# Three spectra exchanged by matmul instead of by DMA, in a gated sum of two spectral filters, under a new instruction list

## The chip, the cores and the metric

One core of a Trainium2 chip runs the whole program in one launch. The metric is the device time of that launch in microseconds. The core has five engines that each run their own instructions in order and wait for each other by semaphores: TensorE (PE, matmul; its weight loads are shown as PEld), VectorE (DVE), ScalarE (ACT), GpSimd (POOL) and SyncE (SP, which here only issues DMAs). Matmuls write to PSUM, an accumulation memory of eight banks that GpSimd cannot read; everything else lies in SBUF, the 128-partition working memory.

## The reference

```python
def reference(A_x, A_w_r, A_w_i, B_x, B_w_r, B_w_i, gate_w):
    x = A_x                                   # (1, 2048, 1024) bf16
    g = sigmoid((x * gate_w).sum(-1, keepdims=True))
    a = irfft2(rfft2(x) * (A_w_r + 1j*A_w_i)) # over both axes, W is (2048, 513)
    b = irfft2(rfft2(x) * (B_w_r + 1j*B_w_i))
    return g * a + (1 - g) * b                # bf16
```

Two filters act on the same two-dimensional spectrum of x, and a gate per row mixes the two results.

## The kernel before, in words

Both transforms are matrix products with constant cosines and sines. The 2048 rows are split as 32 x 64, so that the forward transform goes in steps; the work is cut into *jobs*, each a small function that adds one or a few instructions.

- **fold, egen, s1m, s1e**: stage 1. x arrives in eight groups (load.x.g.half), is folded or reversed (fold), and meets a constant E (two halves, load.E) of which egen makes signed copies. s1m.g.j are eight matmuls into one PSUM unit, s1e.g.j evicts that unit into F1 (line 458). There are 16 of these pairs.
- **s2m, s2e, s4m, s4e**: for each of 16 values t (in the order 1 to 12, 0, 13, 14, 15) eight matmuls transform along the columns (s2m), an eviction stores to one of three CS buffers (s2e), four matmuls with constants from CK finish the row transform (s4m, line 490), and an eviction gives the spectrum X(t) (s4e, line 498). Partition 2k holds the real, 2k+1 the imaginary part.
- **swap, xneg**: the complex product needs the spectrum with real and imaginary rows exchanged as well. swap(t) does it with two DMAs from SBUF to SBUF (line 502), into S(t). xneg(t) makes the copy with alternating signs (line 507), XN(t); the second half of XN(t) overwrites the first half of S of the spectrum four steps earlier, so it waits until that has been read by prod2.
- **prod1, prod2, pm**: the products with the weights W, read from memory in chunks (load.W), on VectorE. prod1 reads XN, prod2 reads S. Block 0 is the low 256 columns for one t (blocks 3 and 4 are its halves); pm does the high columns for several t at once.
- **gwm, gwe, gsm, gse, rowsum, zsm, zse, zst, zld**: the gate: a few matmuls beside stage 2, sums over t, a sigmoid, a round trip through memory into SI.
- **stm, ste, stp, stx, c0m, c0e**: the one column at the Nyquist frequency and column 0, put in order separately.
- **s5m.g, s5e.g** (g = 0 to 31): sixteen small matmuls and an eviction each turn the products round. s5m of g below 16 waits for the low products, of g from 16 for the first half, and of g from 24 for the second half of the pm products.
- **rb**: multiplies the inverse constants U5 by the gate SI. There are eight, for four groups of rows and two parts (cs) each; s6m.p needs both parts of its rows.
- **s6m, s6e, s7m, s7c, s7p, fin, store**: the inverse transform by blocks of rows i = 0 to 15. s7c copies half of a PSUM unit, s7p adds and subtracts on VectorE, fin combines the two halves, store writes out. The mode per i is `"QDQQDQQDQQDQQHHH"`; in mode D (i = 1, 4, 7, 10) s7p writes part of its result into PSUM. PQ, what fin reads, is a ring of four.

Two things set the order of the work. One is the written list ORDER (line 19): its jobs are emitted in that order, each engine runs its own in list order, and a suffix names the engine (a ScalarE, d VectorE, p GpSimd, s SyncE; the same letter on load, swap and store names the queue). The other is the helper that turns what each job reads and writes into semaphore waits; PSUM is four units that are handed out in the order in which the list gives them back (lines 333 to 342).

```python
def take(*key):
    unit_of[key] = free.pop(0)
    return unit_of[key]
```

All matmuls are recorded on line 330, ScalarE's copies on 316 and with signs on 325, VectorE's casts on 318, sign passes on 327, products and rb on 321, DMAs on 312, egen.1.2 on 425, folds on 436, s7p on 728, 729 and 737, fin on 747.

Of the kernel before, what the change touches and what calls it, by code (L numbers as in the profile page):

```python
# [18 lines left out]
ORDER = """
load.SM.a load.x.0.1.s load.x.1.1.s zero load.x.0.0.a load.E.0.a load.x.1.0.s load.x.2.0.a load.x.2.1.s wf.5 wf.1 wf.4 load.E.1.s fold.0.1.p  # L20
wf.2 tbl fold.0.0.d warm.10x512x1 load.x.4.0.s egen.0.1 fold.1.0.d load.x.4.1.a fold.1.1.d s1m.0.1 load.x.7.0.s s1m.0.0 fold.2.1.d
fold.2.0.d load.GR.p s1m.1.1 egen.1.3 egen.1.1 load.x.6.1.a load.x.7.1.a load.x.5.1.s load.x.6.0.a fold.4.0.d s1e.0.1.a s1m.1.0 wf.3
s1e.1.1.a s1m.2.1 wf.6 egen.1.2 rev s1e.2.1.a s1m.4.1 s1m.4.0 load.x.5.0.s s1e.1.0.d s1e.0.0.a load.VC.p fold.7.0.d load.x.3.0.s s1m.2.0
load.x.3.1.s s1m.7.0 fold.6.0.d load.F2.s s1e.4.0.a load.W.9.4.s fold.5.0.p s1m.6.0 load.CK.s s1e.2.0.d s1m.6.1 s1e.4.1.a fold.3.0.d
s1e.7.0.a s1e.6.0.a s1m.5.1 s1e.6.1.a fold.3.1.d s1m.5.0 s1e.5.1.a s1m.3.0 s1e.5.0.d s1m.7.1 s1m.3.1 gwm s1e.3.0.a s1e.7.1.d s1e.3.1.a s2m.1
s2e.1.a s2m.2 gwe.a load.W.24.4.s s2m.3 load.W.0.5.s s2e.3.a s2e.2.d s4m.1 s4e.1.a s2m.4 s4m.2 s2m.6 load.W.28.4.s s4m.3 s2e.4.a gsm.1.4
xneg.1.a s4e.2.d s4m.4 load.W.5.4.s gse.1.4.a swap.1.s s2e.6.d s4e.3.a swap.2.a s4e.4.d xneg.3.a s2m.5 swap.3.s s2m.7 s2e.7.a s2m.9 s4m.6
s2e.5.d gsm.5.4 swap.4.a load.W.20.4.s xneg.4.d s2e.9.a s4m.7 prod1.3.0.d gse.5.4.a prod1.4.0.d s4e.6.a s4m.5 prod2.1.0.d s2m.10 gsm.0.1
swap.6.s s4e.7.a prod2.3.0.d prod2.2.0.d s4e.5.a s4m.9 xneg.6.d prod1.1.0.d s2e.10.a s2m.8 xneg.2.p swap.7.a gse.0.1.a swap.5.s xneg.7.d
s2e.8.a load.W.16.4.s s4m.10 s4e.10.a s4e.9.a s2m.11 s4m.8 s4e.8.a gsm.9.4 gse.9.4.a s2e.11.a prod2.4.0.d xneg.5.d prod1.2.0.d swap.9.s  # L30
gsm.13.3 swap.8.a prod1.7.0.d s2m.12 prod1.5.0.d prod2.6.0.d prod1.6.0.d swap.10.s load.W.13.3.s prod2.5.0.d xneg.10.d xneg.9.d prod2.7.0.d
s2e.12.a xneg.8.d s2m.0 prod1.9.0.d s4m.11 gse.13.3.a s2e.0.a prod1.8.0.d s4m.12 rowsum.0.p s4e.12.a s4e.11.d s4m.0 s2m.13 swap.12.s stm
s2m.14 s4e.0.a swap.11.s xneg.11.d rowsum.1.d prod2.8.0.d rowsum.2.d s2e.13.a prod2.9.0.d xneg.12.d xneg.0.d prod1.12.0.d prod1.11.0.d
s2m.15 s2e.14.a prod2.10.0.d s4m.13 s2e.15.a prod2.12.0.d prod1.10.0.d prod1.0.3.d prod1.0.4.d s4m.15 ste.d s4e.13.a s4m.14 zsm swap.0.s
s4e.15.a stp.2 swap.13.s s4e.14.a xneg.15.a xneg.13.d prod2.11.0.d prod2.0.0.d stp.1 prod1.13.0.d swap.14.a prod2.13.3.d stx.p swap.15.s
prod1.15.4.d prod1.15.3.d zse xneg.14.a prod1.14.3.d prod2.15.3.d prod2.14.3.d prod1.14.4.d s5m.5 prod2.13.4.d s5e.5.a prod2.15.4.d
pm.1.0.0.13.3.d pm.1.1.0.9.7.d pm.1.1.1.9.7.d s5m.1 s5m.3 s5e.1.a s5m.7 s5e.3.a s5m.6 prod2.14.4.d zst.p s5e.7.a s5m.14 s5m.2 pm.1.0.0.5.8.d
s5e.6.a stp.0 s5e.14.a pm.1.1.1.1.8.d pm.1.0.1.1.4.d s5m.12 pm.1.0.1.13.3.d s5m.8 pm.1.0.1.5.8.d prod2.0.1.d c0m s5e.2.a c0e.d s5e.8.a
s5e.12.a s5m.9 pm.1.1.0.1.8.d s5m.0 pm.1.0.0.1.4.d s5m.4 s5e.9.a pm.2.1.1.9.7.d prod1.0.2.d s5m.13 s5m.15 s5e.0.a prod1.0.1.d pm.2.0.0.5.8.d
s5e.15.a pm.2.0.1.13.3.d s5m.10 s5e.10.a s5m.11 s5m.19 s5e.4.a s5e.11.a prod2.0.2.d pm.2.0.1.1.4.d s5e.13.a s5m.22 s5e.22.a s5m.17 zld.s  # L40
s5e.19.a s5m.23 s5e.23.a s5m.21 pm.2.1.0.1.8.d s5e.21.a pm.2.0.0.13.3.d pm.2.1.0.9.7.d pm.2.1.1.1.8.d pm.2.0.0.1.4.d pm.2.0.1.5.8.d s5m.20
load.U5.0.s s5m.16 s5e.20.a s5e.17.d s5m.18 s5m.27 load.U5.1.s s5e.18.a s5m.26 s5m.28 s5e.16.d rb.0.4.1.p s5e.27.a s5e.26.d s5e.28.a s5m.24
s5m.31 s5m.29 s5m.30 s5e.24.d s5m.25 s5e.31.a rb.0.4.0.p load.DI.s s5e.29.a s5e.30.d s5e.25.a s6m.0.0 rb.4.4.0.d s6m.1.0 s6m.0.1 rb.4.4.1.d
s6e.0.0.a s6e.1.0.a s6m.1.1 rb.8.4.0.d s6e.0.1.a s6m.2.0 s7m.0 rb.12.4.1.d rb.8.4.1.d s7c.0.a s6e.1.1.d s7m.1 rb.12.4.0.d s6e.2.0.a
s7p.0.0.d s7p.0.1.d fin.0.1.p fin.0.0.p s7c.1.a s7m.2 s7c.2.a s7p.1.1.d s6m.2.1 s6m.3.1 s7p.2.0.d s7p.2.1.d s7m.3 s6e.2.1.a s7p.1.0.d
s6m.3.0 s6e.3.1.a fin.1.0.d s7c.3.a fin.1.1.d fin.2.1.p s7m.4 store.0.0.a s6e.3.0.a s7c.4.a s7p.3.0.d s7p.3.1.d s7p.4.1.d s7m.5 s7c.5.a
s6m.4.0 fin.2.0.p s6m.4.1 s7p.5.0.d s7p.5.1.d s7m.6 s7p.4.0.d s6e.4.0.a s6e.4.1.a fin.3.0.p s7c.6.a fin.4.0.d s7m.7 s6m.5.0 store.0.1.a
fin.4.1.d fin.3.1.p fin.5.1.p store.1.1.s s6m.5.1 store.3.0.s store.2.0.s fin.5.0.p s7c.7.a store.1.0.a s7p.6.0.d s7p.6.1.d s6e.5.0.a
s7p.7.1.d s7p.7.0.d s7m.8 s6e.5.1.a fin.7.0.d s7m.9 s6m.6.0 s7c.8.a fin.7.1.d store.5.0.a s7c.9.a s7p.8.0.d s7p.8.1.d store.2.1.s
store.4.0.s s6m.6.1 s7m.10 s6e.6.0.a store.7.0.a s7p.9.0.d s6m.7.0 fin.6.1.p fin.6.0.p store.3.1.p s7p.9.1.d s7c.10.a store.6.0.a fin.8.1.p  # L50
s7m.11 s7p.10.1.d s6e.6.1.a s7m.12 s7p.10.0.d s6e.7.0.a store.5.1.s store.7.1.s fin.10.0.d fin.8.0.p s7c.11.a s6m.7.1 fin.9.0.p fin.10.1.d
fin.9.1.p s7p.11.0.d s7p.11.1.d s7c.12.a store.8.0.a s6e.7.1.a store.4.1.a store.6.1.s s7m.13 fin.11.0.d s7p.12.0.d fin.11.1.p s7c.13.a
s7p.12.1.d fin.12.0.p fin.12.1.p store.8.1.a store.10.0.a store.10.1.s s7m.14 store.9.1.s s7c.14.a store.9.0.s store.11.1.a store.12.1.p
s7m.15 store.11.0.a s7p.13.0.d s7p.13.1.d s7p.14.0.d s7c.15.a store.13.0.a s7p.14.1.d s7p.15.0.d s7p.15.1.d store.13.1.s store.14.1.s
store.12.0.p store.14.0.a store.15.0.s store.15.1.a
"""


# [202 lines left out]
def bass_gated_mix__spectral_gfnet__spectral_gfnet__prompt_kernel(nc, A_x, A_w_r, A_w_i, B_x, B_w_r, B_w_i, gate_w, out):  # L261
# [52 lines left out]
    def copy(eng, dst, src, **kw):  # L314
        if eng == "act":
            P.add("act", lambda e: e.activation(dst, src, ACT.Copy), **kw)  # L316
        else:
            P.add(eng, lambda e: e.tensor_copy(dst, src), **kw)  # L318
# [4 lines left out]
    def sign(eng, dst, src, col, **kw):  # L323
        if eng == "act":
            P.add("act", lambda e: e.activation(dst, src, ACT.Copy, scale=SM[:, col:col + 1]), **kw)  # L325
        else:
            P.add(eng, lambda e: e.tensor_scalar(out=dst, in0=src, scalar1=SM[:, col:col + 1], scalar2=None, op0=ALU.mult), **kw)  # L327

    def mm(o, lh, rh, first, last, **kw):
        P.add("pe", lambda e: e.matmul(o, lh, rh, start=first, stop=last), **kw)  # L330
# [500 lines left out]
```

## Time and profile before

| | us |
|---|---|
| runs shown | 123.19 (median), 127.07, 123.03 |
| profiled execution | 122.19 |
| its span, first to last instruction | 120.4 |
| busy: PE, DVE, ACT, POOL | 102.4, 101.5, 91.9, 42.6 |
| mean granted TensorE clock | 0.972 of full speed |

The page of the profile gives busy time by engine, the chain of work that ended last, and groups of instructions by line and shape: "x30" is a count, a bracket with an arrow names what ended the idle time ahead of an instruction. A merged row of the timeline gives the start of the first instruction, the time to the end of the last and their number. Consecutive instructions of one engine overlap a little, so that the spacing from start to start is shorter than the duration of one.

### The profile page before, as it was taken

How to read it: one execution, taken by the hardware profiler on the slowest of the kernel's cores; microseconds unless marked ns; L12 is line 12 of the kernel's file. 1: busy time of each engine (PE TensorE's matmuls, PEld its weight loads, DVE VectorE, ACT ScalarE, POOL GpSimd, SP SyncE). 2: the span in 40 equal slices, each digit the busy share in tenths (PEclk: the TensorE clock that was granted, in tenths of full speed). 3: DMA queues.
4: the chain of work that ended last, by engine and by line, in shares of the span. 5: the costliest groups of instructions: out<-in, count | busy, mean ns of one | idle time of the engine just before them, and what ended most of it. 6: DMA issues, size and time to landing. Idle time of an engine off the chain costs nothing.

```text
span 120.4 us, 3373 instructions
## 1 busy us (share of the span) xinstructions
PE 102.4 (85%) x1387; PEld 81.4 (68%) x1395; DVE 101.5 (84%) x165; ACT 91.9 (76%) x111; POOL 42.6 (35%) x40
## 2 busy tenths in 40 slices
...
GB/s 30 343 353 384 380 420 407 419 420 415 391 302 320 283 277 308 290 166 251 16 0 5 166 338 155 419 155 0 5 0 5 21 66 89 265 204 62 265 198 238
DMA packets 13535, 26.58 MB, mean 221 GB/s; under 512 B 2288, under 2 KB 6416, under 8 KB 13136
## 3 DMA queue, kind: packets, MB, share of 16 engines
...
q0 software_dynamic: 384, 0.55, 1.3%
...
## 4 chain that ended last, share of the span: by engine, by line
PE 55%; DVE 29%; DMA 5%; POOL 3%; ACT 2%; issue 2%; SPq 1%; POOLq 0%
PE PS L330 55%; DVE PF L321 23%; DMA PF<-in_A_x_dram 5%; POOL PF L747 2%; ACT PF L316 2%; DVE PF L318 1%; DVE PF L327 1%; SPq L312 1%; DVE PF L436 1%; DVE WA L318 1%; ACT PF L425 1%; DVE AT L595 0%; POOL out_dram L312 0%; POOLq L770 0%; DVE PST L321 0%
## 5 line engine op out<-in xcount | busy, mean ns | idle before, releaser
L316 ACT ACTIVATE PF<-PS 128x1024 bf16<-128x1024 f32 (+1 forms) x69 | 59.7, 929 | 15.0 <-PE PS L330 13.7
L330 PE MATMUL PS<-PF 128*128 128x256 bf16 (+2 forms) x404 | 51.2, 281 | 4.1 <-POOL PF L358 1.3
L330 PEld LDWEIGHTS PS<-PF 128*128 128x128 bf16 x406 | 36.5, 99 | 16.4 <-issue 2.4
L321 DVE TENSOR_TENSOR PF<-PF,WA 128x1024 bf16<-128x1024 bf16 (+4 forms) x62 | 39.8, 706 | 0.1
L330 PE MATMUL PS<-CK,PF 128*128 128x64 bf16 x512 | 21.4, 204 | 7.9 <-DVE PF L321 4.8
L316 ACT ACTIVATE WA<-PS 128x1024 bf16<-128x1024 f32 x27 | 25.3, 1062 | 3.5 <-PE PS L330 3.4
L330 PEld LDWEIGHTS PS<-CK,PF 128*128 128x128 bf16 x512 | 19.8, 120 | 9.4 <-DVE PF L321 5.3
L747 POOL TENSOR_TENSOR PF<-PF 128x512 bf16<-128x512 f32 x17 | 21.8, 1307 | 9.9 <-DVE PF L737 9.7
L318 DVE CAST PF<-PS 128x1024 bf16<-128x1024 f32 (+1 forms) x12 | 13.8, 1156 | 7.0 <-PE PS L330 6.9
L330 PE MATMUL PS<-PF,CK 128*128 128x512 bf16 (+2 forms) x66 | 15.7, 357 | 0.9 <-ACT PF L316 0.3
L330 PE MATMUL PS<-PF,WA 128*128 128x128 bf16 x256 | 15.6, 219 | 0.0
L737 DVE TENSOR_TENSOR PF<-PS,PF 128x512 f32<-128x512 f32 (+1 forms) x24 | 15.1, 680 | 0.3
L330 PEld LDWEIGHTS PS<-PF,WA 128*128 128x128 bf16 x256 | 14.9, 98 | 0.2
L321 POOL TENSOR_TENSOR PF<-PF 128x1024 bf16<-128x1024 bf16 x2 | 6.1, 3078 | 20.4 <-DMA PF<-c_U 20.4
L330 PEld LDWEIGHTS PS<-PF,CK 128*128 128x128 bf16 x72 | 6.4, 97 | 6.3 <-ACT PF L316 1.5
L436 DVE TENSOR_TENSOR PF<-PF 128x1024 bf16<-128x1024 bf16 x7 | 4.5, 689 | 4.7 <-DMA PF<-in_A_x_dram 4.6
L327 DVE TENSOR_SCALAR PF<-PF,SM 128x1024 bf16<-128x1024 bf16 x14 | 7.5, 552 | 0.9 <-DMA PF<-c_E 0.8
L327 POOL TENSOR_SCALAR PF<-PF,SM 128x1024 bf16<-128x1024 bf16 x1 | 2.8, 2846 | 12.5 <-DVE PF L318 12.5
L321 POOL TENSOR_TENSOR VT<-VC,GSB 128x512 f32<-128x512 bf16 x1 | 1.2, 1161 | 14.5 <-ACT GSB L316 14.5
L318 DVE CAST WA<-PS 128x1024 bf16<-128x1024 f32 x5 | 5.8, 1218 | 0.2 <-PE PS L330 0.2
L747 DVE TENSOR_TENSOR PF<-PS,PF 128x512 bf16<-128x512 f32 x8 | 5.1, 685 | 0.1
L325 ACT ACTIVATE PF<-PF,SM 128x1024 bf16<-128x1024 bf16 x4 | 4.6, 1148 | 0.3 <-ACT PF L316 0.3
...
## 6 DMA issues: line engine op xcount, KB each, us to landing
PF<-PF SPq DMA_DIRECT2D x22, 128.0 KB, 3.0
PF<-in_A_x_dram SPq DMA_DIRECT2D x10, 256.0 KB, 7.8
PF<-c_U SPq DMA_DIRECT2D x2, 1024.0 KB, 5.2
out_dram<-PF ACTq DMA_DIRECT2D x15, 128.0 KB, 2.2
out_dram<-PF SPq DMA_DIRECT2D x14, 128.0 KB, 2.1
...
```

What stands on the lines that cost most here:

```text
L312: return P.add(eng, lambda e: e.dma_start(dst, src), dma=name, **kw)
L316: P.add("act", lambda e: e.activation(dst, src, ACT.Copy), **kw)
L318: P.add(eng, lambda e: e.tensor_copy(dst, src), **kw)
L321: P.add(eng, lambda e: e.tensor_tensor(out=dst, in0=s0, in1=s1, op=ALU.mult), **kw)
L325: P.add("act", lambda e: e.activation(dst, src, ACT.Copy, scale=SM[:, col:col + 1]), **kw)
L327: P.add(eng, lambda e: e.tensor_scalar(out=dst, in0=src, scalar1=SM[:, col:col + 1], scalar2=None, op0=ALU.mult), **kw)
L330: P.add("pe", lambda e: e.matmul(o, lh, rh, start=first, stop=last), **kw)
L425: P.add("act", lambda e: e.activation(sl(PF, EO + 4096 + o, [(1, n)]), src, ACT.Copy, scale=-1.0), r=[("E", c)], a=[("EG", c)])
L436: P.add(Q[eng], lambda e: e.tensor_tensor(out=fs, in0=xs(0, 1), in1=xs(511, -1), op=ALU.subtract if k else ALU.add), **kw)
L737: P.add(Q[eng], lambda e: e.tensor_tensor(out=o, in0=ps(u * 1024, [(1, 512)]), in1=eos(i), op=op), r=[("EO", i % 2)] + banks(u)[:1], **kw)
L747: P.add(Q[eng], lambda e: e.tensor_tensor(out=od, in0=a0, in1=pv[:, :, 1, :], op=ALU.subtract if s else ALU.add), r=kr, a=XALL + [("OU", i ...
```

## The change

Four new jobs and one new buffer replace the exchange by DMA for t = 13, 14 and 15. CKX is a copy of the eight transform constants with neighbouring columns exchanged (ckx, made once). s4x(t) is s4m with CKX in place of CK, so that its result has real and imaginary rows exchanged; s4y(t) evicts it straight to S(t). s4n(t) evicts the ordinary s4m result with alternating signs, by ScalarE's scale operand, straight to XN(t). The three s4e, xneg and swap of these t are gone. s1h evicts one half of a stage 1 unit; s1m.3.1 is now evicted by ScalarE (one bank) and VectorE (the other). ORDER is new throughout: other engines for some jobs, another order for most.

```diff
+    CKX = sb("CKX", 512)
...
+    def s1h(g, j, b, eng):
+        u = unit_of["s1", g, j] if b == 0 else give("s1", g, j)
+        copy(Q[eng], sl(PF, FTo + j * 512 + 4 * g + 2 * b, [(1024, 16), (32, 16), (1, 2)]), ps(u * 1024 + 512 * b, [(16, 16), (1, 16), (256, 2)]),
+             r=banks(u)[b:b + 1], a=[("F1", t) for t in range(16)])
...
-    def s4m(t):
+    def s4m(t, *x):
         kind = 0 if t else 1
-        u = take("s4", t)
+        u = take("s4", t, *x)
         for pm in range(2):
             for k in range(2):
...
+                o = FB[kind, pm, k]
+                lh = sl(CKX if x else CK, o, [(1, 128)])
...
+    def ckx(eng):
+        copy(Q[eng], CKX[:], sl(CK, 1, [(2, 256), (-1, 2)]), r=["CK"], w=["CKX"])
+
+    def s4x(t):
+        s4m(t, 1)
+
+    def s4y(t, eng):
+        u = give("s4", t, 1)
+        copy(Q[eng], sl(PF, So(t), [(256, 2), (512, 2), (1, 256)]), ps(u * 1024, [(512, 2), (256, 2), (1, 256)]), r=banks(u), a=[("F1", t), ("XS", t)])
+
+    def s4n(t, eng):
+        u = give("s4", t)
+        k = [("XS0", STEPS[POS[t] - LAGX])] if POS[t] >= LAGX else []
+        sign(Q[eng], sl(PF, XA(t), [(256, 2), (XB(t) - XA(t), 2), (1, 256)]), ps(u * 1024, [(512, 2), (256, 2), (1, 256)]), 1,
+             r=["SM"] + banks(u), w=[("XN", NI[t]), ("XN1", t)] + k)
```

The list has 503 jobs before and 505 after. Engine by engine, the stretches that matter here (before in "-", after in "+"):

```diff
 SP, start
-load.x.0.1 load.x.1.1 load.x.1.0 load.x.2.1 load.E.1 load.x.4.0 load.x.7.0 load.x.5.1 load.x.5.0 load.x.3.0 load.x.3.1
+load.x.1.1 load.x.1.0 load.E.0 load.E.1 load.x.2.0 load.x.6.1 load.x.6.0 load.x.7.1 load.x.3.0 load.x.3.1
 ACT, start to the end of stage 1
-load.SM load.x.0.0 load.E.0 load.x.2.0 tbl load.x.4.1 load.x.6.1 load.x.7.1 load.x.6.0 s1e.0.1 s1e.1.1 egen.1.2 s1e.2.1 s1e.0.0 s1e.4.0 s1e.4.1 s1e.7.0 s1e.6.0 s1e.6.1 s1e.5.1 s1e.3.0 s1e.3.1
+load.x.0.1 load.SM load.x.0.0 tbl load.x.2.1 load.x.4.1 load.x.4.0 load.x.7.0 load.x.5.1 load.x.5.0 egen.1.2 s1e.0.0 s1e.1.0 s1e.0.1 s1e.1.1 s1e.2.0 s1e.4.1 s1e.4.0 s1e.6.1 s1e.6.0 s1e.5.0 s1e.5.1 s1h.3.1.0 s1e.3.0
 DVE, start to the first product
-fold.0.0 egen.0.1 fold.1.0 fold.1.1 fold.2.1 fold.2.0 egen.1.3 egen.1.1 fold.4.0 s1e.1.0 fold.7.0 fold.6.0 s1e.2.0 fold.3.0 fold.3.1 s1e.5.0 s1e.7.1 s2e.2 s4e.2 s2e.6 s4e.4 s2e.5 xneg.4 prod1.3.0
+fold.1.0 fold.1.1 fold.0.0 fold.0.1 egen.0.1 egen.1.1 egen.1.3 fold.2.0 fold.2.1 s1e.2.1 fold.6.0 fold.7.0 fold.5.0 fold.3.0 fold.3.1 s1e.7.0 s1e.7.1 s1h.3.1.1 gwe s2e.1 s2e.2 s2e.4 s4e.2 xneg.1 xneg.2 s4e.4 xneg.4 s2e.5 xneg.3 prod1.1.0
 PE, behind stage 1
-s2m.1 s2m.2 s2m.3 s4m.1 s2m.4 s4m.2 s2m.6 s4m.3 gsm.1.4 s4m.4 s2m.5 s2m.7 s2m.9 s4m.6
+s2m.1 s2m.2 s2m.3 s2m.4 s4m.1 s4m.2 s4m.3 s4m.4 gsm.1.4 s2m.5 gsm.13.3 s2m.7 s2m.6 s4m.5
 PE, end of stage 4
-s2m.13 stm s2m.14 s2m.15 s4m.13 s4m.15 s4m.14 zsm s5m.5
+stm s2m.13 s2m.15 s2m.14 s4m.13 s4x.15 s4m.15 s4x.13 s4x.14 s4m.14 zsm s5m.5
 ACT, end of stage 4
-s2e.13 s2e.14 s2e.15 s4e.13 s4e.15 s4e.14 xneg.15 swap.14 zse xneg.14 s5e.5
+s2e.13 s2e.15 s2e.14 s4n.13 s4y.15 s4n.15 s4y.13 s4y.14 s4n.14 zse s5e.5
 DVE, ahead of the first s5m
-ste stp.2 xneg.13 prod2.11.0 prod2.0.0 stp.1 prod1.13.0 prod2.13.3 prod1.15.4 prod1.15.3 prod1.14.3 prod2.15.3 prod2.14.3
+prod2.12.0 ste prod1.0.4 prod2.11.0 prod1.13.0 prod2.15.3 rowsum.2 prod1.15.4 prod1.15.3 stp.2 prod2.13.3 prod2.0.0 prod2.14.3 stp.0 stp.1 prod1.14.3
 DVE, behind the last product
-s5e.17 s5e.16 s5e.26 s5e.24 s5e.30 rb.4.4.0 rb.4.4.1 rb.8.4.0 rb.12.4.1 rb.8.4.1 s6e.1.1 rb.12.4.0 s7p.0.0
+s5e.13 s5e.23 s5e.26 s5e.24 s5e.25 rb.4.4.1 s6e.1.0 rb.8.4.1 s7p.0.0
 PE, around the last product
-s5m.18 s5m.27 s5m.26 s5m.28 s5m.24 s5m.31 s5m.29 s5m.30 s5m.25 s6m.0.0 s6m.1.0 s6m.0.1
+s5m.13 s5m.23 s5m.27 s5m.17 s5m.26 s5m.28 s5m.24 s5m.31 s5m.30 s5m.25 s5m.29 s6m.1.0 s6m.0.0 s6m.0.1
 POOL, whole, without the first loads
-fold.0.1 rev fold.5.0 xneg.2 rowsum.0 stx zst rb.0.4.1 rb.0.4.0 fin.0.1 fin.0.0 fin.2.1 fin.2.0 fin.3.0 fin.3.1 fin.5.1 fin.5.0 fin.6.1 fin.6.0 store.3.1 fin.8.1 fin.8.0 fin.9.0 fin.9.1 fin.11.1 fin.12.0 fin.12.1 store.12.1 store.12.0
+fold.4.0 rev zst rb.0.4.0 rb.0.4.1 rb.4.4.0 rb.8.4.0 rb.12.4.0 rb.12.4.1 fin.0.1 fin.0.0 fin.2.1 fin.3.1 fin.2.0 fin.3.0 fin.5.1 fin.6.1 fin.5.0 fin.6.0 fin.8.0 fin.8.1 fin.9.0 fin.9.1 fin.11.0 fin.11.1 fin.12.0 store.12.0 store.11.1
 SP, behind stage 4
-zld load.U5.0 load.U5.1 load.DI
+stx load.U5.0 load.U5.1 zld load.DI
```

Further moves between engines: gse.5.4, gse.9.4 and rowsum.0 go to VectorE, c0e to ScalarE, fin.11.0 to GpSimd and fin.12.1 to VectorE; xneg.1, 2 and 3 go to VectorE.

78 lines of the change are left out of this document (39 added, 39 removed).

## The prediction

> **What bounds the kernel now.** I read the page's head first, then the chain that ended last in order of time, then the timeline engine by engine to find the instants at which one stage hands over to the next. The head gives the span, the chain the hand-overs (start us, us long, what):
>
> ```profile
> span 120.4 us, 3373 instructions
> ```
>
> ```profile
> 22.04 2.79 PE PS L330 x24
> ...
> 46.34 1.24 DVE PF L318
> ...
> 68.11 0.35 DVE PF L318
> 68.46 11.42 DVE PF L321 x15
> 79.88 1.14 DVE WA L318
> 81.02 0.05 issue
> 81.07 29.77 PE PS L330 x472
> ```
>
> So TensorE sets the pace until VectorE takes over at 46.34; VectorE's products (and the small copy at 68.11, c0e) run to 79.88, TensorE again to the end. The stretch that the change's first part touches, t = 13, 14, 15, lies at 50 to 59. The table by stretch (length, then busy us and count of PE, PEld, DVE, ACT, POOL, then clock, DMA share, GB/s) shows VectorE without a gap there:
>
> ```profile
> 50.00:55.00 5.00, 3.75 (x20) 1.69 (x19) 4.96 (x12) 4.79 (x7) 0.16 (x1) 1.00 0.55 201
> 55.00:59.30 4.30, 0.02 (x1) 0.02 (x2) 4.30 (x12) 2.35 (x5) 1.61 (x3) 0.64 0.43 156
> ```
>
> I cut the span at instants that the timeline names: first product, first s5m, first s5m behind the last product, first s6m.
>
> ```profile
> 33.54 2.72 DVE L321 TENSOR_TENSOR PF<-PF,WA 128x1024 bf16<-128x1024 bf16 x4
> 59.28 2.91 PE L330 MATMUL PS<-CK,PF 128*128 128x64 bf16 x51 [4.48 <-DVE PF L321]
> 80.30 4.88 PE L330 MATMUL PS<-CK,PF 128*128 128x64 bf16 x128 [0.28 <-ACT WA L316]
> 85.02 4.63 PE L330 MATMUL PS<-PF,WA 128*128 128x128 bf16 x80
> ```
>
> Before: (a) 22.04 to the first s2m, (b) 11.50 to the first product, (c) 25.74 to the first s5m, (d) 20.60 to the last product's end T = 79.88, (e) 5.14 to the first s6m, (f) 35.38 to the end. They sum to 120.4; each term is now worked out for the new list.
>
> **The change part by part.** *The exchanged spectra.* Gone are three evictions, three sign passes (two on ScalarE, one on VectorE) and six DMAs of 3.0 us; new are twelve matmuls, six ScalarE copies and one 512-element copy (ckx). Durations from the timeline:
>
> ```profile
> 26.41 1.03 PE L330 MATMUL PS<-PF,CK 128*128 128x512 bf16 x4
> 27.27 1.04 PE L330 MATMUL PS<-PF 128*128 128x256 bf16 x8
> 28.14 1.03 PE L330 MATMUL PS<-PF,CK 128*128 128x512 bf16 x4
> 29.00 0.94 PE L330 MATMUL PS<-GW,PF 128*128 128x2 bf16 x32
> ```
>
> Start to start an s4m is 0.86, an s2m 0.87, a gsm of four takes 0.94; an op's last matmul ends 0.17 behind the next op's start (1.04 against 0.87). Three s4x cost TensorE 2.6 us, inside the 4.48 it idles ahead of 59.28: nothing, by that cover; without it, 2.6. The DMAs' removal gains nothing directly, because VectorE idles 0.04 us between 50 and 59.3: no product waits for a swap. What VectorE gains is one sign pass, counted in (c). ScalarE's s4n (with the sign) is bounded by the sign pass and the plain copy:
>
> ```profile
> L325 ACT ACTIVATE PF<-PF,SM 128x1024 bf16<-128x1024 bf16 x4 | 4.6, 1148 | 0.3 <-ACT PF L316 0.3
> L316 ACT ACTIVATE PF<-PS 128x1024 bf16<-128x1024 f32 x53 | 51.3, 1028 | 11.5 <-PE PS L330 11.5
> ```
>
> I take 1.03 for all six (range 0.93 to 1.15). s4n.14 and s4n.15 wait on the in-order ScalarE for prod2.11 and prod2.12 (their target is those spectra's first half), with s4y behind them and zse last; by the counts of (b) and (c) VectorE reaches both about 1 us ahead of ScalarE (an estimate), so I cost these waits at 0, up to 1 us if VectorE is late. From the first s2m TensorE needs 16 x 0.87 + 13 x 0.86 + 4 x 0.94 + 0.3 = 29.2 until s2m.14 is through; seven ScalarE copies at 1.0 behind it end at 36.4, and VectorE wants s4n.14's result at (b) + (c) less one product, 10.8 + 26.6 - 0.4 = 37.0: free, with 0.6 of cover. ckx (0.6 by half a copy) falls where ScalarE has slack, 15 us ahead of its reader.
>
> *Stage 1 (a).* ScalarE's evictions pace it, and the new list puts egen.1.2, which needs the second E load, ahead of all of them.
>
> ```profile
> 0.72 2.79 SPq L312 DMA_DIRECT2D PF<-in_A_x_dram  x4
> PF<-c_E SPq DMA_DIRECT2D x1, 256.0 KB, 6.8
> 11.02 1.05 ACT L425 ACTIVATE PF<-PF 128x1024 bf16<-128x1024 bf16 x1
> 14.16 6.52 ACT L316 ACTIVATE PF<-PS 128x1024 bf16<-128x1024 f32 x7 [0.26 <-PE PS L330]
> ```
>
> The issues are 0.7 apart, so E's second half, now fourth on the queue, goes out at 2.9 (before: 3.5, fifth) and lands at 9.7 by the same 6.8 us. egen.1.2 ends at 10.75; twelve full evictions at 0.93 start to start and one half (0.55) behind it end at about 22.4; TensorE starts again 0.05 later. Before, two evictions were done ahead of egen.1.2. The halved s1m.3.1 takes 0.4 off ScalarE, but s1e.3.0 still runs whole behind it, so the split saves no more than that. All in all 22.45: (a) +0.4. Bounds: 0 with E landing 0.4 earlier, +1.3 if PSUM units run short while ScalarE drains one at a time. The fold moved from GpSimd to VectorE costs 0.6 there, and the first egen gets it back (last fence of this part).
>
> *First product (b).* It now waits for more: s2m 1 to 5, s4m 1 to 4 and a gsm precede s2e.5 on TensorE, 5 x 0.87 + 4 x 0.86 + 0.94 = 8.7; then 0.2 until VectorE can start, s2e.5 (1.2), xneg.3 (0.45): 10.6; with a short wait for a CS buffer (s2e.4 behind s4m.1) I take 10.8. VectorE's own load fits below: 1.0 to its first input, six casts at 1.14 (the chain's row at 79.88), four sign passes at 0.44 (next fence), 9.6. Against 11.5: (b) -0.7.
>
> *Products to s5m.5 (c).* The same products, less xneg.13, plus gse.5.4, gse.9.4, rowsum.0 (from GpSimd) and stp.0.
>
> ```profile
> 43.00 0.87 DVE L327 TENSOR_SCALAR PF<-PF,SM 128x1024 bf16<-128x1024 bf16 x2
> L321 DVE TENSOR_TENSOR PF<-PF,WA 128x512 bf16<-128x512 bf16 x16 | 5.9, 420 | 0.0
> L737 DVE TENSOR_TENSOR PF<-PS,PF 128x512 f32<-128x512 f32 x18 | 11.4, 680 | 0.1
> 49.20 0.17 DVE L318 CAST ATB<-AT 128x32 bf16<-128x32 f32 x1
> ```
>
> -0.4 + 2 x 0.17 + rowsum.0 between 0.42 and 0.68 (0.6: float output) + 0.2 = +0.7. Waits on spectra: in the new order xneg.8 and gse.9.4 come to VectorE's turn about when TensorE, at the pace above, has their inputs: +0.2, an estimate. (c) +0.9, bounds 0.4 and 1.9 (ScalarE's waits above).
>
> *s5 (d, e).* VectorE has the same products less stp.0 (0.2, an estimate as in (c)) and c0e (0.35): (d) -0.55. Behind T nine s5m are left instead of eight (27, 17, 26, 28, 24, 31, 30, 25, 29), at 4.88 / 8 = 0.6 each, and s5m.13's and s5m.23's units are held until VectorE gets to their copies: (e) +0.55. SP now issues zld behind both U5 loads:
>
> ```profile
> PF<-c_U SPq DMA_DIRECT2D x2, 1024.0 KB, 5.2
> PF<-zd SPq DMA_DIRECT2D x4, 128.0 KB, 2.5
> 65.26 2.65 SPq L312 DMA_DIRECT2D PF<-zd  x4
> ```
>
> U5.1 leaves at about the same place of s5 as before (behind s5m.10, sixteenth); four issues (2.65) and 2.5 us behind it SI is there at about the time at which U5.1 itself lands, 5.2, or up to 1 us behind. That is 77.9 to 79 on before's clock (rb started at 77.9, next fence), still ahead of T, and until T rb cannot run anyway: 0; if it slipped behind T, GpSimd's cover below takes it.
>
> *rb to GpSimd (f).* GpSimd takes six of the eight rb (before: two), VectorE keeps two.
>
> ```profile
> L321 POOL TENSOR_TENSOR PF<-PF x1: 4014/4014/4014, 77.9 to 77.9; 128x1024 bf16<-128x1024 bf16 x1
> L321 POOL TENSOR_TENSOR PF<-PF x1: 2141/2141/2141, 81.8 to 81.8; 128x1024 bf16<-128x1024 bf16 x1
> 76.90 2.98 DVE L321 TENSOR_TENSOR PF<-PF,WA 128x2048 bf16<-128x2048 bf16 x3
> 5.11 2.62 POOL L436 TENSOR_TENSOR PF<-PF 128x1024 bf16<-128x1024 bf16 x1 [3.58 <-DMA PF<-in_A_x_dram]
> L327 DVE TENSOR_SCALAR PF<-PF,SM x14: 475/478/1496, 6.5 to 54.7; 128x1024 bf16<-128x1024 bf16 x14
> 97.37 5.00 POOL L747 TENSOR_TENSOR PF<-PF 128x512 bf16<-128x512 f32 x4 [0.25 <-DVE PF L737]
> 97.40 0.43 DVE L728 TENSOR_TENSOR PS<-PS,PF 128x256 f32<-128x256 f32 x1
> ```
>
> The first rb, beside products, took 4.01: it stood until VectorE's products ended at 79.8 and then ran 2.1. The second, beside PSUM copies, took 2.14. The other way round, the first egen took 1.50 instead of 0.48 while a GpSimd fold ran. So six rb run from T to T + 12.8. s6m.0 and s6m.1 need the first two (T + 4.3, wanted at T + 5.7), s6m.2 the third (T + 6.4, wanted at T + 9.4). fin.0 then needs 2 x 1.25 more: T + 15.3. The D-mode s7p.4.1 (97.40, 12.4 behind the first s6m) overwrites what fin.0 reads and is due at T + 18.1: covered, by 2.8. VectorE's 4 x 0.6 saved gains nothing, since TensorE has no gap from 81.07. But each of VectorE's two rb can stand behind a GpSimd rb for up to 2.14, with s6e.1.0 and s7p.0.0 queued behind. VectorE has its last s5 copy done near T + 6.4; s7p.0.0 is due behind five s6m (85.02's row: 4.6 for 80 matmuls), s7m.0 and its half copy at T + 11.4, and 2.5 of work lies between: 2.4 of slack against 4.3, so 0 to 1.9; I take +0.4, since GpSimd is in an rb for most of that time but both must collide. At the very end fin.12.1 goes from GpSimd to VectorE: -0.2. (f) +0.2.
>
> The Trainium skill, SBUF — State Buffer, "Who interferes with whom", says that a VectorE instruction with two SBUF inputs and a GpSimd instruction that reads SBUF exclude each other for a whole instruction. By that rule, this case's trace agrees (4.01 against 2.14), and the worst price, both collisions, is the upper 1.9.
>
> **Sum:** +0.4 - 0.7 + 0.9 - 0.55 + 0.55 + 0.2 = +0.8 us on the span. The profiled execution took 122.19 (span 120.4 and 1.8 around it), the median shown is 123.19; from the first I get 123.0, from the second 124.0, and forecast the middle, 123.5.
>
> **Rivals** (from the same middle, 122.7). *Faster:* the lists' waits fall better than my count: (a) 0, (c) +0.4, (e) +0.1, (f) -0.2, which with -0.7 and -0.55 gives -0.95: 121.7. For it speaks that before's own waits (0.26 us of ScalarE in stage 1's row above is one of several) are what a new list can remove; against it, that VectorE's work up to T is not less. *GpSimd becomes the bound:* it decides when 6 rb + 2.5 us exceed 18.1, a mean of 2.6 per rb. At 3.08, the mean of the two before, s7p.4.1 is 2.9 late on a VectorE that has no slack from there on: +3.7, 126.4. Against it: behind T only two VectorE instructions there have two SBUF inputs. *Stage 1 and the sign copies late:* (a) +1.3 and (c) +1.9 give +2.7, 125.4. *The matmuls do not do their part:* if exchanging by matmul saved nothing at all, the time would be the same as forecast, since no swap is waited for.
>
> **How the numbers follow.** Forecast 0.55, faster 0.27, GpSimd 0.08, late 0.10. Range: the faster rival with the profiled run's base gives 121.2, rounded in to 121.4; above, the late case, 125.4. Within 2% (2.5 us, about what a measurement of this kernel can tell from no change) lie the forecast, nearly all of the faster case and half of the late one. Faster by over 2% would need T 2.5 us earlier with no term that gives it: 0.07. Slower: 0.08 for GpSimd and 0.05 of the late case, 0.13; the rest, 0.80, is within.
>
> **What would show it.** First s2m behind a start of about 22.4; first product near 33.3; first s5m near 59.9 with TensorE idle less than 4.5 before it; T near 80; nine s5m behind it; first s6m near 85.7; six rb on GpSimd in 13 to 14 us from T; the s7p behind fin.0 not waiting. I am wrong if E lands far from 9.7, if s4n waits for prod2, or if rb runs longer than 2.6.

## The result, and the profile after

The changed kernel took 125.11 us against 124.23 us of the kernel before on the same chip, both medians of four runs. All ratios here leave out runs in which the chip was in a slower state (one of the changed kernel's four, two of the other's, six of e9's twelve), and the traces of e6 and e9, taken in that state, are not read. What remains, 125.02, 124.80 and 125.21 against 123.19 and 123.03, gives a ratio of 1.0154, 95% interval [1.0112, 1.0197]. Timed again in twelve runs (below, e14) it was 1.0109 [1.0075, 1.0143], medians 124.52 us against 122.99 us. So it is slower, by 1.1% to 1.5%; 0.65% was forecast (+0.8 us on the profiled 122.19 us). Every ratio is taken against runs of the kernel before on the same chip.

The profiled execution after took 125.02 us. I cut its span at the instants at which the prediction cut the old one. T is read as the start of VectorE's first copy behind the last product (79.80 in before, where the prediction had 79.88, so that its (d) and (e) shift by 0.08). The last column is a second trace of the same kernel.

| term | before | predicted | after | after again (e14) |
|---|---|---|---|---|
| (a) to the first s2m | 22.04 | 22.45 | 23.57 | 25.36 |
| (b) to the first product | 11.50 | 10.8 | 10.81 | 10.81 |
| (c) to the first s5m | 25.74 | 26.6 | 27.87 | 26.44 |
| (d) to T | 20.52 | 20.0 | 20.08 | 20.06 |
| (e) to the first s6m | 5.22 | 5.8 | 5.21 | 5.23 |
| (f) to the end | 35.38 | 35.6 | 35.66 | 35.60 |
| span | 120.4 | 121.2 | 123.2 | 123.5 |

The chain that ended last, after (start us, us long, what):

```profile
2.14 6.85 DMA PF<-in_A_x_dram
...
23.57 3.67 PE PS L331 x32
...
35.39 1.03 ACT PF L317
...
46.31 4.49 DMA PF<-PF
...
62.79 19.62 DVE PF L322 x26
82.46 27.00 PE PS L331 x452
```

From 62.79 the chain is as before: VectorE's products, then TensorE. It differs ahead of that. Before's chain began with a load of x too (from 2.20, 5.92 long, waited for by fold.1); this one takes 6.85 and is x.0.0, waited for by fold.0. New are a ScalarE copy at 35.39 and a swap transfer at 46.31. These links lie in (a) and (c), where the time went.

**Stage 1.** The timelines of ScalarE (its queue, then its instructions) and of VectorE, after:

```profile
0.74 0.71 ACTq L313 DMA_DIRECT2D PF<-in_A_x_dram  x1
1.50 0.61 ACTq L313 DMA_DIRECT2D SM<-c_SM  x1
2.14 0.67 ACTq L313 DMA_DIRECT2D PF<-in_A_x_dram  x1
...
9.51 1.06 ACT L426 ACTIVATE PF<-PF 128x1024 bf16<-128x1024 bf16 x1 [5.18 <-DMA PF<-c_E]
11.42 12.10 ACT L317 ACTIVATE PF<-PS 128x1024 bf16<-128x1024 f32 x13 [0.85 <-PE PS L331]
```

```profile
7.14 1.29 DVE L437 TENSOR_TENSOR PF<-PF 128x1024 bf16<-128x1024 bf16 x2 [6.27 <-DMA PF<-in_A_x_dram]
9.01 1.29 DVE L437 TENSOR_TENSOR PF<-PF 128x1024 bf16<-128x1024 bf16 x2 [0.58 <-DMA PF<-in_A_x_dram]
10.22 1.27 DVE L328 TENSOR_SCALAR PF<-PF,SM 128x1024 bf16<-128x1024 bf16 x3
```

egen.1.2 starts at 9.51, when E's second half is there. But ScalarE then waits another 0.85 for TensorE: x.0.0, third on ScalarE's queue, lands at 8.99, VectorE folds it at 9.01 and only behind that makes egen.0.1 (10.22), which every s1m needs. From 11.42 ScalarE evicts without a gap, twelve whole units and a half, and the first s2m follows at 23.57.

**The products.** ScalarE around the four DMAs of swap.1 and swap.2, then what VectorE waited for between its first product and the first s5m (engine, line, releaser: us in total, times, longest):

```profile
31.83 3.51 ACTq L313 DMA_DIRECT2D PF<-PF  x4
35.39 1.94 ACT L317 ACTIVATE PF<-PS 128x1024 bf16<-128x1024 f32 x2 [3.39 <-PE PS L331]
```

```profile
DVE PF L322 <- DMA PF<-PF: 0.6, 2, 0.3
DVE GSB L319 <- PE PS L331: 0.5, 1, 0.5
DVE PF L328 <- ACT PF L317: 0.5, 1, 0.5
```

In the list before, swap.1 went out on SyncE. ScalarE issued the two DMAs of swap.2 partly beside a copy, and the sign pass behind them waited 0.27:

```profile
30.31 0.53 ACTq L312 DMA_DIRECT2D PF<-PF  x1
30.37 1.02 ACT L316 ACTIVATE PF<-PS 128x1024 bf16<-128x1024 f32 x1
30.87 0.74 ACTq L312 DMA_DIRECT2D PF<-PF  x1
31.66 1.15 ACT L325 ACTIVATE PF<-PF,SM 128x1024 bf16<-128x1024 bf16 x1 [0.27 <-ACT PF L316]
```

Now four are issued in a row, 3.51 us, and s2e.7 and s2e.6 stand behind them; the row names TensorE as their releaser, but the copy starts 0.05 behind the last issue. What follows from the late copies are VectorE's waits for ScalarE and TensorE. By stretch (length, then busy us of PE, PEld and DVE), for (c) before and (c) after:

```profile
33.54:59.28 25.74, 20.03 (x209) 13.14 (x212) 25.18 (x52) 21.85 (x29) 2.92 (x4) 0.94 0.73 254
```

```profile
34.38:62.25 27.87, 23.58 (x209) 14.80 (x211) 25.98 (x55) 24.64 (x30) 0.30 (x1) 1.00 0.62 209
```

VectorE idles 0.56 of 25.74 before and 1.89 of 27.87 after: +1.33 of waits where +0.2 was taken.

### The profile page after: what moved, and what is told of

Read it like the earlier page. It is cut to its first block, busy times and chain, and to the rows that moved or that the text cites. A ratio compares the mean times of both kernels' runs of the same rounds, so it can differ in the third digit from the quotient of the medians.

```text
span 123.2 us, 3394 instructions
## 1 busy us (share of the span) xinstructions
PE 104.7 (85%) x1401; PEld 81.6 (66%) x1407; DVE 101.9 (83%) x168; ACT 90.7 (74%) x109; POOL 42.5 (34%) x38
## 4 chain that ended last, share of the span: by engine, by line
PE 46%; DVE 26%; DMA 9%; ACT 8%; issue 3%; ACTq 3%; POOL 0%; POOLq 0%; SPq 0%
PE PS L331 46%; DVE PF L322 24%; ACT PF L317 8%; DMA PF<-in_A_x_dram 6%; DMA PF<-PF 4%; ACTq L313 3%; DVE PF L328 1%; POOL out_dram L313 0%; DVE PF L771 0%; POOLq L794 0%; DVE PF L437 0%; SPq L313 0%; DVE PST L322 0%; DVE XST L328 0%; DVE ATB L319 0%
## 5 line engine op out<-in xcount | busy, mean ns | idle before, releaser
L317 ACT ACTIVATE PF<-PS 128x1024 bf16<-128x1024 f32 (+2 forms) x70 | 59.4, 922 | 16.3 <-PE PS L331 14.2
L331 PE MATMUL PS<-CK,PF 128*128 128x64 bf16 x512 | 20.4, 198 | 5.9 <-DVE PF L322 3.8
L331 PEld LDWEIGHTS PS<-CK,PF 128*128 128x128 bf16 x512 | 18.6, 118 | 7.6 <-DVE PF L322 4.2
L771 POOL TENSOR_TENSOR PF<-PF 128x512 bf16<-128x512 f32 x17 | 21.2, 1281 | 1.5 <-DVE PF L761 0.9
L322 POOL TENSOR_TENSOR PF<-PF 128x1024 bf16<-128x1024 bf16 x6 | 14.4, 2427 | 18.8 <-DMA PF<-zd 18.8
L313 POOL DMA_DIRECT2D zd<-ZG x1 | 0.6, 632 | 41.6 <-ACT ZG L659 41.6
L437 DVE TENSOR_TENSOR PF<-PF 128x1024 bf16<-128x1024 bf16 x8 | 5.2, 688 | 7.6 <-DMA PF<-in_A_x_dram 7.6
L319 POOL COPY PF<-PF 128x1024 bf16<-128x1024 bf16 x1 | 1.3, 1317 | 11.0 <-DMA PF<-in_A_x_dram 11.0
L331 PEld LDWEIGHTS PS<-GW,PF 128*128 128x128 bf16 x128 | 3.9, 96 | 1.9 <-ACT PF L317 1.4
```

The costliest lines, as they stand in the source:

```text
L313: return P.add(eng, lambda e: e.dma_start(dst, src), dma=name, **kw)
L322: P.add(eng, lambda e: e.tensor_tensor(out=dst, in0=s0, in1=s1, op=ALU.mult), **kw)
L437: P.add(Q[eng], lambda e: e.tensor_tensor(out=fs, in0=xs(0, 1), in1=xs(511, -1), op=ALU.subtract if k else ALU.add), **kw)
L771: P.add(Q[eng], lambda e: e.tensor_tensor(out=od, in0=a0, in1=pv[:, :, 1, :], op=ALU.subtract if s else ALU.add), r=kr, a=XALL + [("OU", i ...
```

## The experiments

Three theories stood at the start. **A:** the loss lies in the list, in stage 1 and in the waits of (c); A1 is its part with the swaps on ScalarE's queue, A2 its part with the loads of stage 1. **B:** the exchange by matmul itself costs. **C:** the six rb on GpSimd cost. In the short diffs "-" is the kernel that the experiment starts from.

**e1, stage 1 as before.**

```diff
-the new jobs up to the last eviction of stage 1, s1h.3.1.0 and s1h.3.1.1
+those of the list before, in its order, s1e.3.1 whole; from s2m.1 on the new list
```

> The changed kernel with stage 1 (loads of x and E, folds, sign copies, s1m, s1e, without the split eviction) in the order of the kernel before; everything behind it as changed. Theory A (the new list's stage 1 starts late, and VectorE waits more for spectra in the products; exchange and rb cost nothing): first s2m back from 23.6 to about 22.0, the whole 1.4 us shorter, about 123.6 us, 0.4% slower than before. Rival B (the exchange by matmul costs: s4n waits for prod2 on the in-order ScalarE) and rival C (six rb on GpSimd) both expect less than 0.4 us, about 124.9 us.

123.49 us, ratio 1.0041 [1.0005, 1.0078], (a) 22.71: about two thirds of the loss is in stage 1.

**e2, the exchange alone, on the kernel before.**

```diff
-s4e.13 s4e.15 s4e.14, their xneg and swap
+ckx, s4x, s4y and s4n of 13, 15 and 14, at the same place of the list before
```

> The kernel before with the exchange alone: ckx, s4x, s4y and s4n for t = 13, 14, 15 in place of s4e, xneg and swap, the rest of its list untouched. Theory A: within 0.5 us of before, 123.1 plus or minus 0.5, since no product waited for these swaps; one sign pass less on VectorE gives at most -0.4. Rival B: slower by 1 us or more, 124.1 or above, with VectorE idle ahead of prod1.14.3.

123.81 us, 1.005 [1.0013, 1.0086]. The price is in (c), 26.60 against 25.74: VectorE reaches the last product before ScalarE has s4n.14.

```profile
56.12 1.94 ACT L315 ACTIVATE PF<-PS 128x1024 bf16<-128x1024 f32 x2 [0.23 <-PE PS L329]
57.95 1.12 ACT L324 ACTIVATE PF<-PS,SM 128x1024 bf16<-128x1024 f32 x1
```

```profile
59.10 6.09 DVE L320 TENSOR_TENSOR PF<-PF,WA 128x512 bf16<-128x512 bf16 x11 [0.81 <-ACT PF L324]
```

So B holds with half a per cent on the old list, where the order gives ScalarE's copies no cover.

**e3, the exchange undone in the changed kernel.**

```diff
-ckx; s4x, s4y, s4n of 13, 15, 14
+s4e, swap and xneg of 13, 15, 14
```

> The changed kernel with the exchange undone: s4e, xneg and two DMAs for t = 13, 14, 15 again, the rest as changed. Theory A: as the changed kernel, 125.0 plus or minus 0.5, or slower where the DMAs now end late. Rival B: faster by 1 us or more, 124.0 or below.

126.63 us, 1.0276 [1.0216, 1.0337]: slower than the changed kernel, not faster, so B is false for this list: there the matmuls save 1.2% (1.0276 / 1.0154) to 1.7% (1.0276 / 1.0109). Where, the trace shows in part. VectorE waits for the transfers of 13 and 15, whose products stand earlier in the new order (first row: 0.39; another 0.17 at 63.00), and has one sign pass more, 0.4. A wait of 2.1 for TensorE lies upstream of the edit, where the granted clock was low (second fence, a stretch of 4 us: 0.61, where the first trace after had 1.00); it is one execution's, and I don't count it for either theory. But all four runs of e3 show a low mean granted clock (0.939 to 0.965, against 0.95 to 0.999 in the changed kernel's), so how much of the 1.2% to 1.7% is the exchange itself is not shown.

```profile
60.49 0.43 DVE L320 TENSOR_TENSOR PF<-PF,WA 128x512 bf16<-128x512 bf16 x1 [0.39 <-DMA PF<-PF]
```

```profile
36.00:40.00 4.00, 3.78 (x47) 2.03 (x47) 3.20 (x7) 2.81 (x5) 0.00 (x0) 0.61 0.89 330
```

**e4, four rb back to VectorE.**

```diff
-rb.4.4.0.p rb.8.4.0.p rb.12.4.0.p rb.12.4.1.p
+the same on VectorE, each beside its neighbour
```

> The changed kernel with four rb back on VectorE (GpSimd has two again). Theory A: no faster than the changed kernel, 125.0 to 125.5, since GpSimd ends its rb at T + 13.4 and nothing on the last chain waits for it there. Rival C: faster by 0.7 us or more, 124.3 or below, with s7p.0.0 less than 5.7 us behind the first s6m (before: 5.7, changed: 5.7).

125.04 us, 1.0118 [1.0042, 1.0194]; (f) 35.70 against 35.66. C is false.

**e5, swap.1 and swap.2 moved to SyncE.**

```diff
-swap.1.a swap.2.a
+swap.1.s swap.2.s ahead of swap.3.s
```

> The changed kernel with swap.1 and swap.2 issued by SyncE, ahead of swap.3, instead of by ScalarE. In the changed kernel's trace these four issues hold ScalarE for 3.5 us, 1.5 of them past the end of s2m.7. Theory A1 (this hold makes the spectra behind it late, and so most of VectorE's extra waits between first product and first s5m): s2e.7 about 1.4 us earlier behind the first s2m, that stretch 27.9 to about 27.0, the whole 0.8 to 1.0 us faster than the changed kernel, about 124.1. Rival (the waits come from the matmul order): within 0.4 of the changed kernel, 124.7 to 125.2.

127.77 us, 1.0354 [1.0276, 1.0433]: A1 fell in this form. SyncE's queue, then what VectorE waited for in (c):

```profile
31.05 5.91 SPq L311 DMA_DIRECT2D PF<-PF  x8
37.00 0.60 SPq L311 DMA_DIRECT2D WA<-in_A_w_r_dram  x1
...
39.62 5.62 SPq L311 DMA_DIRECT2D PF<-PF  x6
```

```profile
DVE PF L320 <- DMA PF<-PF: 3.7, 5, 1.8
DVE PF L320 <- ACT PF L324: 1.0, 1, 1.0
```

ScalarE was free 1.5 us earlier, but SyncE issues eight DMAs in 5.91, and a W load and the later swaps stand behind them. VectorE's wait for transfers grew from 0.6 to 3.7. The queue that was relieved was not the only full one.

**e6, egen.1.2 behind the first evictions.**

```diff
-egen.1.2 ahead of all s1e
+egen.1.2 behind s1e.1.0
```

> The changed kernel with egen.1.2 behind two of ScalarE's evictions, as before, loads as changed. Theory A2 (stage 1 starts late because the halves of x group 0 and 1 and of E land later in the new load order): no gain, first s2m still at 23 to 24, 124.8 to 125.4. Rival (ScalarE's sign copy, put first, holds the evictions, as the prediction had it): first s2m about 1 us earlier, 124.0 or below.

125.24 us, 1.0137 [1.0058, 1.0217]: no gain. The step on which the prediction spent (a), egen.1.2 in front, isn't the cause.

**e7, the first loads and folds as before.**

```diff
-ACT x.0.1 SM x.0.0 ..., SP x.1.1 x.1.0 E.0 ...; fold.1.0 fold.1.1 fold.0.0 fold.0.1 egen.0.1
+ACT SM x.0.0 E.0 ..., SP x.0.1 x.1.1 x.1.0 ...; fold.0.0 fold.0.1 egen.0.1 fold.1.0 fold.1.1
```

> The changed kernel with the first six loads and the first folds in the order of before, egen.1.2 still ahead of the evictions. Theory A2: TensorE's first s1m at 7.5 to 8.5 instead of 10.8, but the evictions then wait for egen.1.2 at 11.4, so that the first s2m gains only 0 to 0.6 us: 124.4 to 125.0. If the load order is all there is: first s2m at 22.2, 123.6.

123.37 us, 1.0031 [0.9986, 1.0076]: this alone gives back most of the loss, more than I expected. x.0 now lands first:

```profile
4.97 1.29 DVE L435 TENSOR_TENSOR PF<-PF 128x1024 bf16<-128x1024 bf16 x2 [4.10 <-DMA PF<-in_A_x_dram]
7.31 0.48 DVE L326 TENSOR_SCALAR PF<-PF,SM 128x1024 bf16<-128x1024 bf16 x1 [1.05 <-DMA PF<-c_E]
```

```profile
9.53 1.06 ACT L424 ACTIVATE PF<-PF 128x1024 bf16<-128x1024 bf16 x1 [5.41 <-DMA PF<-c_E]
10.49 12.08 ACT L315 ACTIVATE PF<-PS 128x1024 bf16<-128x1024 f32 x13
```

egen.0.1 is made at 7.31 instead of 10.22, an s1m is done before egen.1.2 ends, and the same 13 evictions start at 10.49 instead of 11.42: (a) 22.63.

**e8, e1 and e5 together.**

```diff
-stage 1 of the changed kernel; swap.1.a swap.2.a
+stage 1 as in e1; swap.1.s swap.2.s
```

> The changed kernel with before's stage 1 and with swap.1 and swap.2 on SyncE: both repairs together. Theory A and A1: 122.3 to 122.9, at or a little below before. Rival (the extra work on VectorE is the rest of it): not below 123.4.

124.2 us, 1.0107 [1.0019, 1.0195], worse than e1's 1.0041, though the intervals overlap. VectorE's waits for transfers in (c) are 2.0 where e1 has none: moving the swaps to SyncE makes the transfers late here too.

**e9, swap.2 behind s2e.7, still on ScalarE's queue.** Theory H: ScalarE's hold, not the queue's load, is what costs.

```diff
-swap.1.a ... swap.2.a ... s2e.7.a
+swap.1.a ... s2e.7.a swap.2.a
```

> The changed kernel with swap.2 issued behind s2e.7 instead of ahead of it on ScalarE's queue, so that ScalarE issues two DMAs, copies, and issues two more, as before's list does, and SyncE gets no more to do than in the changed kernel. Theory H (what (c) lost lies in ScalarE's hold of 3.39 us while it issues four DMAs): s2e.7 starts some 1.2 us earlier, the 0.46 that VectorE waits for ScalarE and part of the 0.52 for TensorE go, (c) 27.1 to 27.4 instead of 27.87, ratio to the changed kernel's time 0.994 to 0.996. Rival D (the transfers set VectorE's pace there, as with swap.1 and swap.2 on SyncE): swap.2 lands later, VectorE's wait for DMA grows from 0.6 by as much as its other waits fall, (c) 27.7 to 28.2, no gain.

124.37 us, 1.0051 [1.0009, 1.0093] where the changed kernel has 1.0154 and 1.0109: a gain of 0.6% to 1.0%, as H had it, but the interval overlaps that of 1.0109, and the medians of all runs, 124.37 against 122.78, show no gain over e14's 124.52 against 122.99. So e9 alone does not settle it.

**e10, small work back from VectorE.**

```diff
-gse.5.4.d gse.9.4.d rowsum.0.d
+gse.5.4.a gse.9.4.a rowsum.0.p; rowsum.1 behind prod2.8
```

> The changed kernel with gse.5.4 and gse.9.4 on ScalarE and rowsum.0 on GpSimd, as before, and rowsum.1 some ten VectorE instructions later so that it does not wait for GpSimd. Theory W (VectorE's own work sets (c), so that the 0.94 us of these three are paid in full): (c) 26.9 to 27.1, the time 0.6% to 0.8% less than the changed kernel's. Rival: VectorE merely waits longer for its next input, (c) 27.6 to 27.9, no gain.

124.29 us, 1.0115 [1.0071, 1.0158], no difference from the changed kernel; (c) was 27.44, between the two guesses. What VectorE didn't do, it waited:

```profile
DVE PF L326 <- ACT PF L315: 1.3, 2, 0.7
```

**e11, e7 + e9 + e10.**

```diff
-the changed kernel
+the edits of e7, e9 and e10
```

> The changed kernel with the first six loads and folds in before's order, swap.2 behind s2e.7, and gse.5.4, gse.9.4 on ScalarE, rowsum.0 on GpSimd. If the three causes add: (a) 22.6, (b) 10.8, (c) 26.2 to 26.6, the rest as in the changed kernel, span 120.6 to 121.1, device time 122.2 to 122.7, 0.3% to 0.7% less than before. If the waits of (c) only move (rival D): (c) 26.9 to 27.3, 123.1, the same as before.

123.69 us, 1.0042 [0.9996, 1.0088]; (c) 26.77. VectorE waited 1.60 in one place, for the transfer of spectrum 6.

**e12, that wait filled.**

```diff
-prod2.6 prod2.7 prod2.5 ... prod2.8 rowsum.1
+prod2.5 rowsum.1 prod2.6 prod2.7 ... prod2.8
```

> The last kernel (the changed kernel with before's first loads and folds, swap.2 behind s2e.7, gse.5.4, gse.9.4 on ScalarE, rowsum.0 on GpSimd) with prod2.5 and rowsum.1 put ahead of prod2.6, where VectorE waited 1.60 for the transfer of spectrum 6. Theory: that work (two times 0.6) fills the wait, (c) 25.5 to 25.8, span 120.1 to 120.5, 0.4% to 0.7% less than before. Rival: another transfer is as late, the wait moves behind it, (c) 26.5 to 26.8, the same time as the last kernel.

123.29 us, 0.9984 [0.9947, 1.0021]. Of its trace's (c), 27.09, 2.0 are waits for transfers in three places, and prod2.5 itself waited 1.07: the wait moved, as the rival had it. Whether the ratio, better than e11's on another chip by 0.6% with the intervals overlapping, is a gain stays open.

**e13, e7 + e9 without e10.**

```diff
-the changed kernel
+the edits of e7 and e9
```

> The changed kernel with before's first loads and folds and swap.2 behind s2e.7, nothing else. If the two add: (a) 22.1 to 22.8, (c) 26.9 to 27.1, span 120.9 to 121.6, 1.2% to 1.6% less than the changed kernel in this call. If the gain of the earlier start is given back behind it: (c) 27.4 to 27.9.

123.09 us, 0.9974 [0.9935, 1.0013], beside e14 on the same chip a gain of 1.3% (0.9974 / 1.0109). ScalarE's queue and copies, and VectorE's only wait in (c):

```profile
31.94 1.28 ACTq L311 DMA_DIRECT2D PF<-PF  x2
33.99 1.02 ACT L315 ACTIVATE PF<-PS 128x1024 bf16<-128x1024 f32 x1 [1.88 <-PE PS L329]
34.00 1.14 ACTq L311 DMA_DIRECT2D PF<-PF  x2
```

```profile
DVE GSB L317 <- PE PS L329: 0.3, 1, 0.3
```

Two edits of the list (six loads with four folds and egen.0.1, and one swap) take away all that the change had lost; what is left is not distinguishable from the kernel before. No version ran faster than the kernel before by more than its interval. The trace does not divide the gain: its (a), 23.69, is above and its (c), 26.24, below what I expected, and the granted clock was low in its stage 1 (0.63 from 12 to 16 us; see e14). Beside e7's ratio, 1.0031, the place of swap.2 is worth 0.6% with the intervals overlapping.

**e14, the changed kernel again.**

```diff
 no edit
```

> The changed kernel again, unchanged, as the measure for the others of this call. If x.0.0's place on ScalarE's queue makes the landing vary, (a) is anywhere from 22.6 to 24.7, as in the seven kernels with these loads so far, and (b) to (f) are as in its first trace within 0.3; if the first trace was an odd one, (a) is near 22.6.

124.52 us, 1.0109 [1.0075, 1.0143]. Its trace has (a) 25.36 and (c) 26.44, outside both guesses of the text: (a) above 24.7, and (c) 1.43 shorter than in the first trace, so (a) and (c) vary from one execution to the next. x.0 was folded at 9.52; the swaps' issues took 2.55:

```profile
9.52 1.29 DVE L437 TENSOR_TENSOR PF<-PF 128x1024 bf16<-128x1024 bf16 x2 [0.42 <-DMA PF<-in_A_x_dram]
```

```profile
33.62 2.55 ACTq L313 DMA_DIRECT2D PF<-PF  x4
36.22 1.94 ACT L317 ACTIVATE PF<-PS 128x1024 bf16<-128x1024 f32 x2 [2.43 <-PE PS L331]
```

Only 0.51 of the 1.79 by which this (a) is longer than the first trace's lies ahead of the first s1m (11.27 against 10.76). The other 1.28 lies behind it and goes with the granted clock, 0.57 from 12 to 16 us where the first trace had 1.00. The page gives that clock in 40 slices of about 3.1 us (9 is 90% or more), first trace, then e14:

```profile
PEclk9999999999999999999999999999999999999998
```

```profile
PEclk9999599999999999999976999599999999999996
```

The traces must therefore be compared at the same clock. With after's loads in their order, those with 1.00 from 8 to 24 us (after, e3, e5, e10) have (a) at 23.57, 22.68, 23.56, 22.62, a mean of 23.1; e4 and e14, with 0.89, have 24.65 and 25.36. With before's loads, those with 1.00 (before, e1, e2, e7, e8, e11, e12) have 22.04, 22.71, 22.17, 22.63, 22.15, 22.76, 22.36, a mean of 22.4; e13, with 0.89, has 23.69. From the first s1m to the first s2m it is 12.8 to 13.1 in the four, 13.9 and 14.1 in e4 and e14. Why the clock fell is not shown: TensorE had stood idle 2.98 and 3.49 ahead of the first s1m in e4 and e14 and at most 2.67 in the four, which would make it a second price of a late x.0, but in e13 it fell after an idle time of 0.88.

## Why the prediction was wrong

The direction was right and the size was not: the sum was +0.8, the ratios give 1.3 to 1.9 us. The two traces give +2.8 and +3.1, because the profiled execution of before, 122.19, lies below the medians of its later runs, 122.78 to 123.08. Step by step:

- **(a), "All in all 22.45: (a) +0.4": mis-sized.** E landed as predicted (9.5 against 9.7), and twelve and a half evictions took 12.10 against 11.7. The step that failed is that they start when egen.1.2 ends. They start when the first s1m is done, and that hangs on x.0.0's place in ScalarE's queue by way of fold.0, egen.0.1 and VectorE's order. I priced E and never asked when x.0.0 lands. Measured +1.53 and +3.32; of the second, 1.28 goes with the granted clock in stage 1, which no term of the sum had. At a clock of 1.00 the means above differ by 0.7 between the two load orders, and e7 gained 0.8% to 1.2% by this order alone.
- **(b) -0.7: right**, -0.69 in both traces.
- **(c) +0.9: the term "waits on spectra: +0.2" was mis-sized, and not steadily.** The work was about right: 25.98 busy against 25.18, +0.8 where +0.7 was taken. The waits were +1.33 in the first trace and +0.25 in the second (0.81 idle, one wait of 0.5 in it), where the four issues ended earlier behind s2m.7. I had counted TensorE's pace for xneg.8 and gse.9.4 and not what swap.1 and swap.2 do to ScalarE's queue; e9 puts that at 0.6% to 1.0%, and e13 beside e7 at 0.6%, both with overlapping intervals.
- **s4n's waits.** s4n.15 did wait, 0.79 for VectorE, as I had said would make me wrong. It cost nothing: s4n.14 ended at 61.51 and VectorE came to its product at 61.78. In e2, with another order, the same copies cost 0.81. "Free, with 0.6 of cover" was close, 0.27.

```profile
57.43 1.11 ACT L326 ACTIVATE PF<-PS,SM 128x1024 bf16<-128x1024 f32 x1 [0.79 <-DVE XST L319]
...
60.39 1.12 ACT L326 ACTIVATE PF<-PS,SM 128x1024 bf16<-128x1024 f32 x1
```

- **(d) -0.55: right**, -0.44.
- **(e) +0.55: wrong, nothing was lost.** The rows below are TensorE at T, then its first s6m. Nine s5m took 5.08 from their start to the first s6m (0.56 each, not 0.6), and they started 0.13 behind T where before it was 0.50: VectorE's copies, which I had said would hold two units, did not hold TensorE up.

```profile
82.46 5.24 PE L331 MATMUL PS<-CK,PF 128*128 128x64 bf16 x144 [0.74 <-DVE PF L322]
87.54 4.63 PE L331 MATMUL PS<-PF,WA 128*128 128x128 bf16 x80
```

- **(f) +0.2 and the GpSimd rival: right**, +0.28 and +0.22. The six rb took 14.38, a mean of 2.4 and so below the 2.6 that would have made GpSimd the bound. fin.0 ended at 98.25, T + 15.9 where I had T + 15.3, and s7p.4.1, which overwrites what it reads, started at 99.93 without a wait: covered, by 1.7 where I had 2.8. The collision with VectorE that I priced is there, without effect on the end:

```profile
81.39 14.38 POOL L322 TENSOR_TENSOR PF<-PF 128x1024 bf16<-128x1024 bf16 x6 [18.81 <-DMA PF<-zd]
95.73 2.52 POOL L771 TENSOR_TENSOR PF<-PF 128x512 bf16<-128x512 f32 x2
```

```profile
88.33 0.83 DVE L322 TENSOR_TENSOR PF<-PF 128x1024 bf16<-128x1024 bf16 x1
...
90.22 1.48 DVE L322 TENSOR_TENSOR PF<-PF 128x1024 bf16<-128x1024 bf16 x1
93.27 1.29 DVE L761 TENSOR_TENSOR PF<-PS,PF 128x512 f32<-128x512 f32 x2 [1.58 <-ACT PF L317]
...
99.93 0.43 DVE L752 TENSOR_TENSOR PS<-PS,PF 128x256 f32<-128x256 f32 x1
```

VectorE's rb.8.4.1 took 1.48 while GpSimd was in an rb; in e4, beside no rb of GpSimd, four of VectorE's took 2.48 together. s7p.0.0 behind it still waited for ScalarE, not for VectorE. By the rule of the Trainium skill that the prediction named (SBUF — State Buffer, "Who interferes with whom") the 1.48 is what one would see; this trace agrees, and the slack swallowed it.

- **The other rivals.** "Stage 1 and the sign copies late" was the right place with a wrong second half: stage 1 came late, but what was late in (c) were copies behind DMA issues, not the sign copies. "The matmuls do not do their part" has two answers: on the old list they cost 0.5% (e2), on the new one their removal costs 1.2% to 1.7% (e3), the low clock of e3's runs included.

What is shown: the load order and the place of swap.2 account together for the whole loss (e13 beside e14), and that the load order alone gives most of it back (e7). What is not: the size of swap.2's share; why the same queue place lets VectorE fold x.0 at 7.80 in one execution (e3) and at 9.52 in another (e14); why the granted clock falls in stage 1 of some executions; and why the issues on ScalarE are long in one and short in another.
